# Packed attention and two MoE layers on one core: the first MoE's cosine argument carried in turns

## The chip, the cores and the metric

The kernel runs on one core of one Trainium2 chip. The metric is the device time of one execution in microseconds (us); the kernel before was run three times, with a median of 1744.01 us (1743.73 to 1751.22). The engines are named as the profile names them: PE is TensorE's matmul, PEld its weight load, DVE is VectorE, ACT is ScalarE, POOL is GpSimd, SP is SyncE.

## The reference

Eight batches of eight heads with 576 tokens go through an attention by way of 32 packs, and the 4608 tokens of 512 features that come out go through two MoE layers of 2048 inner features.

```python
def sm_attn(qq, kk, vv):                     # scale = 1/sqrt(64)
    s = scale * np.matmul(qq, kk.transpose(0, 1, 3, 2))
    s = s - np.max(s, axis=-1, keepdims=True)
    a = np.exp(s)
    return np.matmul(a / (np.sum(a, axis=-1, keepdims=True) + 1e-09), vv)

p_packed = sm_attn(p, k, v)
x = sm_attn(q, p_packed, p_packed)           # then tokens x (heads * 64)

h = x @ w_in                                 # first MoE
y = (h * np.cos(h)) @ w_out

h = y @ w2_in                                # second MoE
P = a[0] + a[1] * h + a[2] * h * h + a[3] * h * h * h
Q = 1.0 + np.abs(b[0]) * np.abs(h) + np.abs(b[1]) * h * h
out = (P / (Q + 1e-6)) @ w2_out
```

## The kernel before

Every float32 operand of a matmul is carried as two parts, hi and lo, and a product takes three matmuls (`PASSES`). The weights come as 64-bit words and are made into the two parts by `convert` (L74 to L93: Sign and Abs on ACT, four integer and float steps on DVE, two products on POOL, a copy on ACT).

The work falls into three stages. In the first, the packs attend to the tokens, and `wunit` (L279) multiplies the pooled packs with the first MoE's `w_in`, so that W' stands in for the second attention product and `w_in` together; W' leaves PSUM in `wev` (three of four pieces by ACT at L296, one by DVE at L294) and goes to HBM.

The second stage is the first MoE. Its 128 slots (8 batches, 2 halves of 288 tokens, 8 pairs of feature blocks) run in the loop of L609. A slot does 12 matmuls of 288 columns into h (`mm_h`, L530), the chain that makes g = h cos h out of them (`chain1`), and the 24 matmuls that add g to y (`mm_y`, L574) for the slot two back. h lies in two PSUM buffers (bufs=2), each of which comes free when the last reader of the chain, L561, is done. The chain is: L554 on ACT (u = h/(2 pi) + 0.25), L555 on DVE (u rounded by adding and taking away 1.5 * 2^23), L556 on DVE (r = h - 2 pi u), L560 on ACT (Sin of r + pi/2), L561 on DVE (g = h r). Then `finish_g` splits the g of the slot before into gh (L66, ACT) and gl (L67, DVE). Beside this the same engines do the second attention of the next batch (`attn2_steps`, whose splits run on POOL too), the splits of the next batch's W' (POOL), the conversion of the rest of `w_out` at the start, and from slot 16 on one conversion of the second MoE's weights every third slot (`conv_w2`).

The third stage is the second MoE (from L649), whose chain is another one.

The order on each engine is not written out by hand: the tile framework orders the instructions when it builds the program, from their dependencies, their place in the code and its own estimate of times, and each engine then runs its list in that order. Some instructions are held behind the latest matmul of `mm_h` (`hold`).

Of the kernel before, what the change touches and what calls it, by code (L numbers as in the profile page):

```python
# [12 lines left out]
AF = mybir.ActivationFunctionType  # L13
ALU = mybir.AluOpType
# [6 lines left out]
def pack_attention_moe_moe_kernel(  # L21
# [14 lines left out]
    nc = tc.nc  # L36
# [11 lines left out]
    scale = 1.0 / math.sqrt(D)  # L48
    RND = 1.5 * 2.0 ** 23
    INV2PI = 1.0 / (2.0 * math.pi)  # L50
    PASSES = ((0, 0), (0, 1), (1, 0))

    # Keeps an instruction behind the matmul `until` in the issue order.
    def hold(ins, until):
        if until is None:
            return
        tc.add_manual_dep(
            ins.ins,
            until.ins.name,
            mybir.DependencyInfo(mybir.DependencyClass.NoSync, mybir.DependencyReason.SCHED_ONLY),  # L60
            reason="issue order",
        )

    # A float32 operand is carried as two float32r parts, x = hi + lo (exact).
    def split(hi, lo, src, lo_eng, until=None):
        hold(nc.scalar.activation(out=hi, in_=src, func=AF.Copy), until)  # L66
        lo_eng.tensor_tensor(out=lo, in0=src, in1=hi.bitcast(F32), op=ALU.subtract)  # L67

    # The weights come as float64 words (viewed as integers).  The word's upper half gives sign,
    # exponent and 20 bits, its lower half the rest; together they give the two float32r parts.  # L70
    def words(w):
        return w.bitcast(U32).rearrange("p (n t) -> p n t", t=2)

# [32 lines left out]
    coef = const.tile([128, 8], F32, name="coef")  # L106
# [1 line left out]
    QC = 1.0 + 1e-6  # L108

    if True:  # L110
# [1 line left out]
        a_p = [ctx.enter_context(tc.tile_pool(name="a0", bufs=1))]  # L112
        RW = dict(reuse_waits="tile")
        wb_p = ctx.enter_context(tc.tile_pool(name="wb", bufs=1, side="right"))
# [27 lines left out]
        def load_kv(n):  # L142
# [10 lines left out]
            out=coef[:, 4:6], in0=par[:, 4:6], scalar1=-1.0, scalar2=None, op0=ALU.mult  # L153
        )
        nc.vector.tensor_tensor(out=coef[:, 4:6], in0=coef[:, 4:6], in1=par[:, 4:6], op=ALU.max)
        nc.vector.memset(coef[:, 6:7], 0.25)
        nc.vector.memset(coef[:, 7:8], math.pi / 2.0)
        nc.vector.memset(par[:, 6:7], QC)
        qb = par[:, 6:7]
# [119 lines left out]
        def wunit(P, hp, fq):  # L279
            ps = ps0.tile([128, 512], F32, tag="w", bufs=2, name="w")  # L280
            wl = wl_t[P]
            for i, (a, c) in enumerate(PASSES):
                nc.tensor.matmul(  # L283
                    out=ps,
                    lhsT=wl[a][:, hp].rearrange("p b m -> p (b m)"),
                    rhs=w1i_s[hp][c][:, 512 * fq:512 * fq + 512],
                    start=(i == 0),
                    stop=(i == 2),
                )
            if fq % 2 == 0:  # L290
                wev_t[P, hp] = wi_p.tile([128, 1024], F32, tag="wev", bufs=3, name="wev")
            o = wev_t[P, hp][:, 512 * (fq % 2):512 * (fq % 2) + 512]
            if fq % 4 == 3:
                nc.vector.tensor_copy(o, ps)  # L294
            else:
                nc.scalar.activation(out=o, in_=ps, func=AF.Copy)  # L296
            if fq % 2 == 1:
                t = wev_t.pop((P, hp))
                g, gg = divmod(hp, 2)
                for b2 in range(2):  # L300
                    nc.scalar.dma_start(
                        out=wd[2 * P + b2][g, 64 * gg:64 * gg + 64, 512 * (fq - 1):512 * (fq + 1)],
                        in_=t[64 * b2:64 * b2 + 64, :],
                    )

# [1 line left out]
        a_t = {}  # L307

        def attn2_steps(b, pool, psp, pst, psb, tg, now):
# [92 lines left out]
        for n in range(NG + 1):  # L402
            if n >= 3:
                next(at, 1)
            if n < NG:
                s1(n)
                if n + 2 < NG:
                    load_kv(n + 2)
            if n >= 1:
                pv(n - 1)  # L410
            for _ in range(2):
                if units:
                    wunit(*units.pop(0))
            if n + 1 < NG:
                prep(n + 1)
            if n < NG:
                et(n)
            for x in range(3 * n, 3 * n + 3):
                if 0 <= x < len(cv1):
                    conv_w1i(x)  # L420
            for _ in range(2):
                if units:
                    wunit(*units.pop(0))
            if n >= 1:
                ppt(n - 1)
                if n % (2 * G) == 0:
                    P = n // (2 * G) - 1
                    units += [(P, hp, fq) for hp in range(H // 2) for fq in range(4)]
# [7 lines left out]
            pass  # L436
        e0a.close()

# [1 line left out]
        e1k = ExitStack()  # L440
        wo_p = ctx.enter_context(tc.tile_pool(name="wq", bufs=1, **RW))
        w1o_s = {}
# [33 lines left out]
            nc.sync.dma_start(out=w2d[0][i], in_=hi.bitcast(F32))  # L476
            nc.sync.dma_start(out=w2d[1][i], in_=lo.bitcast(F32))

        # The second MoE's weights and tokens move in where the first one's leave.
        NB = NT // 512  # L480
        w2_s, x_t, pools = {}, {}, {}

# [57 lines left out]
        def finish_g(n):  # L540
            if n not in gl_t:
                return
            gt = gl_t.pop(n)
            gh = wk.tile([128, 2, HS], F32R, tag="gh", bufs=3, name="gh")
            gl = wk.tile([128, 2, HS], F32R, tag="gl", bufs=3, name="gl")
            split(gh, gl, gt, nc.vector)
            gs_t[n] = (gh, gl)

        def chain1(n):
            ph = h_t.pop(n)[:, :, 0:HS]  # L550
            u = wk.tile([128, 2, HS], F32, tag="u", bufs=2, name="u")
            r = wk.tile([128, 2, HS], F32, tag="r", bufs=2, name="r")
            gt = wk.tile([128, 2, HS], F32, tag="g", bufs=2, name="g")
            nc.scalar.activation(out=u, in_=ph, func=AF.Identity, scale=INV2PI, bias=coef[:, 6:7])  # L554
            nc.vector.tensor_scalar(out=u, in0=u, scalar1=RND, scalar2=RND, op0=ALU.add, op1=ALU.subtract)  # L555
            nc.vector.scalar_tensor_tensor(  # L556
                out=r, in0=u, scalar=-2.0 * math.pi, in1=ph, op0=ALU.mult, op1=ALU.add
            )
            finish_g(n - 1)
            nc.scalar.activation(out=r, in_=r, func=AF.Sin, bias=coef[:, 7:8])  # L560
            nc.vector.tensor_tensor(out=gt, in0=ph, in1=r, op=ALU.mult)  # L561
            gl_t[n] = gt

        def mm_y(n):
# [25 lines left out]
        for f in range(NFC):  # L590
            if f % 4 == 0:
                for _ in range(4):
                    wunit(*units.pop(0))
                load_wq(0, f // 4)
            conv_w1o(f)
            if f + 2 < NFC:
                load_w1o(f + 2)
            if f % 4 == 2:
                split_wq(0, f // 4, nc.gpsimd)
# [9 lines left out]
        for n, (b, hf, j) in enumerate(slots):  # L609
            s = hf * 8 + j  # L610
            mm_h(n)
            chain1(n)
            if n >= 2:
                mm_y(n - 2)
            i2, ph2 = divmod(n - 16, 3)
            if 0 <= i2 < 2 * NFC:
                if ph2 == 0:
                    load_w2(i2)
                elif ph2 == 2:
                    conv_w2(i2)  # L620
            if b + 1 < B:
                if s == 0:
                    at = attn2_steps(b + 1, at_p, psh, "h", 2, {"aT": ("qT", 1)}, lambda: last_h[0])
                if s % 2 == 1:
                    next(at, 1)
                if s == 15:
                    for _ in at:
                        pass
                for jj, (sl, ss) in enumerate(((2, 7), (10, 13), (12, 15), (14, 16))):
                    if s == sl:  # L630
                        load_wq(b + 1, jj)
                    if s == ss:
                        split_wq(b + 1, jj, nc.gpsimd, last_h[0])
            if b > 0 and s == 0:
                split_wq(b, 3, nc.gpsimd, last_h[0])
            move_in(n)
# [9 lines left out]
        for f in range(13, NFC):  # L646
            load_w2s(f, pools["b"])

# [1 line left out]
        slots2 = [(t, f) for t in range(NB) for f in range(NFC)]  # L650
        h2_t, g2_t, o_t = {}, {}, {}

# [127 lines left out]
```

## Time and profile before

| | |
|---|---|
| median of three runs | 1744.01 us |
| the profiled execution's own time (its span) | 1744.9 us |
| TensorE's mean granted clock | 0.973 of full speed |
| busy: PE, DVE, ACT, POOL | 93%, 82%, 67%, 20% of the span |
| first stage, first MoE, second MoE | about 0 to 205, 205 to 930, 930 to 1745 us |

A busy share is that of instructions in work; matmuls overlap, so that a stretch in which PE is busy throughout can still hold more or fewer matmuls. An instruction's busy time on DVE or POOL includes time in which it is started but held. "Idle before, releaser" is the time in which an engine stood still ahead of an instruction, and what ended it.

### The profile page before, as it was taken

The page shows a single profiled execution, that of the slowest core. Times are in us where ns is not written, and L with a number is a line of the kernel's source. Part 1 is how long each engine was busy: PE and PEld are TensorE (multiplying, and loading weights), DVE is VectorE, ACT ScalarE, POOL GpSimd, SP SyncE. Part 2 cuts the span into 40 slices and gives each one's busy share as a digit, 9 for nine tenths or more (in the row PEclk, how much of TensorE's full clock was granted, in tenths as well). Part 3 has the DMA queues.
Part 4 walks back from the last instruction along what each step waited for, and adds up shares of the span by engine and source line. Part 5 has one row for each costly group of instructions (what it writes and reads, how often), then busy time and mean ns, then how long its engine had stood idle before and what let it go on. Part 6 is the DMA issues. An engine that isn't in the chain of part 4 may idle for free.

```text
span 1744.9 us, 24418 instructions
## 1 busy us (share of the span) xinstructions
PE 1619.0 (93%) x8896; PEld 1419.4 (81%) x8896; DVE 1424.5 (82%) x2143; ACT 1175.8 (67%) x1917; POOL 355.0 (20%) x235
## 2 busy tenths in 40 slices
PE   5889578999899989899999999999999999999996
PEld 3668378989899989889898888888888888888884
DVE  6993598798889889988867888888888888888884
ACT  4554566666656566666547787878787878787874
POOL 4650553434334434343300000000000000000000
PEclk9989789999999999999999999999999999999998
DMA  9897822443434434433348020202020202020000
GB/s 291 249 258 234 271 88 83 135 134 113 141 120 134 135 122 136 140 129 107 130 161 304 1 72 1 72 1 73 1 73 1 73 0 72 2 72 1 31 19 25
DMA packets 99768, 183.52 MB, mean 105 GB/s; under 512 B 11584, under 2 KB 46400, under 8 KB 99648
## 3 DMA queue, kind: packets, MB, share of 16 engines
q1 hardware_dynamic: 92224, 163.09, 29.3%
q10 hardware_dynamic: 7424, 18.88, 3.5%
q8 instruction: 70, 1.15, 0.3%
q14 instruction: 50, 0.41, 0.1%
HBM read 117.97 MB, written 63.96 MB: 104 GB/s over the span
## 4 chain that ended last, share of the span: by engine, by line
PE 66%; DVE 20%; ACT 5%; issue 4%; DMA 3%; POOL 1%; SPq 0%; ACTq 0%; DVEq 0%
PE h L659 23%; PE o L718 23%; PE y L574 11%; PE h L530 6%; DVE gl L67 3%; DVE u L555 3%; DVE cvp L89 2%; DVE r L556 2%; DVE cvp L87 2%; DVE g L561 2%; DVE cvf L90 1%; DVE cvf L82 1%; DMA st<-in_moe_w_in_dram 1%; PE w L283 1%; PE s L209 1%
## 5 line engine op out<-in xcount | busy, mean ns | idle before, releaser
L574 PE MATMUL y<-gh,w1o 128*128 128x288 f32 x2048 | 431.8, 297 | 2.3 <-DVE yl L67 2.3
L659 PE MATMUL h<-x,w 128*128 128x512 f32 x1728 | 422.7, 393 | 0.0
L659 PEld LDWEIGHTS h<-x,w 128*128 128x128 f32 x1728 | 324.1, 188 | 74.2
L574 PEld LDWEIGHTS y<-gh,w1o 128*128 128x128 f32 x2048 | 338.1, 190 | 3.8 <-DVE yl L67 3.2
L718 PE MATMUL o<-w,g2h 128*128 128x512 f32 x1152 | 334.0, 394 | 1.3 <-ACT g2h L677 1.3
L574 PE MATMUL y<-gl,w1o 128*128 128x288 f32 x1024 | 298.7, 297 | 15.0 <-DVE gl L67 14.7
L530 PE MATMUL h<-ah,wq 128*128 128x288 f32 x1024 | 236.2, 307 | 46.0 <-DVE g L561 43.2
L718 PEld LDWEIGHTS o<-w,g2h 128*128 128x128 f32 x1152 | 216.0, 188 | 53.1 <-ACT g2h L677 2.1
L530 PEld LDWEIGHTS h<-ah,wq 128*128 128x128 f32 x1024 | 179.5, 197 | 51.0 <-issue 49.4
L574 PEld LDWEIGHTS y<-gl,w1o 128*128 128x128 f32 x1024 | 193.3, 189 | 18.9 <-DVE gl L67 18.9
L718 PE MATMUL o<-w,g2l 128*128 128x512 f32 x576 | 199.9, 393 | 0.0
L693 ACT ACTIVATE sq<-h 128x512 f32<-128x512 f32 x144 | 87.4, 607 | 155.7 <-PE h L659 155.6
L560 ACT ACTIVATE r<-r,coef 128x576 f32<-128x576 f32 x128 | 99.1, 775 | 103.1 <-DVE r L556 102.4
L695 DVE SCALAR_TENSOR_TENSOR ab<-sq,coef,ab 128x512 f32<-128x512 f32 x144 | 108.1, 751 | 67.8 <-ACT ab L694 67.5
L530 PE MATMUL h<-al,wq 128*128 128x288 f32 x512 | 156.1, 305 | 0.0
L67 DVE TENSOR_TENSOR gl<-g,gh 128x576 fp32r<-128x576 f32 x128 | 126.3, 989 | 18.0 <-ACT gh L66 16.3
L704 DVE SCALAR_TENSOR_TENSOR ab<-ab,y 128x512 f32<-128x512 f32 x144 | 99.5, 691 | 48.1 <-ACT y L701 47.5
L91 POOL TENSOR_TENSOR cvf<-cvf,cvs 128x512 f32<-128x512 f32 x64 | 88.2, 1377 | 217.7 <-DVE cvf L90 216.5
L554 ACT ACTIVATE u<-h,coef 128x576 f32<-128x576 f32 x128 | 93.8, 734 | 54.3 <-PE h L530 53.8
L718 PEld LDWEIGHTS o<-w,g2l 128*128 128x128 f32 x576 | 108.0, 188 | 25.6
L696 ACT ACTIVATE c<-h,coef 128x512 f32<-128x512 f32 x144 | 114.1, 792 | 9.8 <-DVE g2l L683 9.8
L561 DVE TENSOR_TENSOR g<-h,r 128x576 f32<-128x576 f32 x128 | 95.9, 750 | 30.1 <-ACT r L560 29.9
(97 smaller groups left out, 2775.6 us busy)
## 6 DMA issues: line engine op xcount, KB each, us to landing
x<-yd SPq DMA_DIRECT2D x36, 512.0 KB
w<-w2d SPq DMA_DIRECT2D x68, 256.0 KB
st<-in_moe_w_in_dram SPq DMA_DIRECT2D x32, 512.0 KB
wd<-wev ACTq DMA_DIRECT2D x64, 256.0 KB
st<-in_moe_w_out_dram SPq DMA_DIRECT2D x32, 512.0 KB
wq<-wd SPq DMA_DIRECT2D x32, 512.0 KB
kx<-in_k_dram SPq DMA_DIRECT2D x16, 576.0 KB
vx<-in_v_dram SPq DMA_DIRECT2D x48, 192.0 KB
```

The lines of the kernel that those rows point to most:

```text
L67: lo_eng.tensor_tensor(out=lo, in0=src, in1=hi.bitcast(F32), op=ALU.subtract)
L91: nc.gpsimd.tensor_tensor(out=ff, in0=ff, in1=sg, op=ALU.mult)
L530: last_h[0] = nc.tensor.matmul(out=ps[:, u, 0:HS], lhsT=wq[:, g, a, o:o + 128], rhs=a_t[b, g][c][:, hf * HS:hf * HS + HS], start=(i == 0), ...
L554: nc.scalar.activation(out=u, in_=ph, func=AF.Identity, scale=INV2PI, bias=coef[:, 6:7])
L560: nc.scalar.activation(out=r, in_=r, func=AF.Sin, bias=coef[:, 7:8])
L561: nc.vector.tensor_tensor(out=gt, in0=ph, in1=r, op=ALU.mult)
L574: nc.tensor.matmul(out=y_t[d][:, 0:HS], lhsT=w1o_s[f // 4][a][:, f % 4, 128 * d:128 * d + 128], rhs=gs[c][:, u], start=(f == 0 and i == 0) ...
L659: nc.tensor.matmul(out=ps, lhsT=w2_s[f][:, 0, a, 128 * kk:128 * kk + 128], rhs=x_t[t, c, kk], start=(i == 0), stop=(i == 3 * NKD - 1),)
L695: nc.vector.scalar_tensor_tensor(out=ab, in0=sq, scalar=coef[:, 5:6], in1=ab, op0=ALU.mult, op1=ALU.add)
L696: nc.scalar.activation(out=c1, in_=ph, func=AF.Identity, scale=coef[:, 3:4], bias=coef[:, 2:3])
L704: nc.vector.scalar_tensor_tensor(out=ab, in0=ab, scalar=QC, in1=y0, op0=ALU.add, op1=ALU.mult)
L718: nc.tensor.matmul(out=o_t[s], lhsT=g2_t[n][a][:, 128 * s:128 * s + 128], rhs=w2_s[f][:, 1, c], start=(f == 0 and i == 0), stop=(f == NFC ...
```

## The change

Three places are touched. In `wunit`, the copies that take W' out of PSUM scale it by 1/(2 pi): the ACT copy gets a scale, the DVE copy becomes a multiplication. All of h in the first MoE is then in turns. In `chain1`, L554 adds 1.5 * 2^23 to h on ACT (no scale, the constant comes from the column of `coef` that held 0.25), so that writing u as float32 rounds it to a whole number; L555 falls away; L556 becomes r = (u - 1.5 * 2^23) - h; a new ACT instruction makes |r|; Sin takes -2 pi |r| + pi/2, which is the cosine; and the last product becomes (2 pi h) * r, as a scalar-tensor-tensor instruction with the same two tensor inputs.

```diff
-        nc.vector.memset(coef[:, 6:7], 0.25)
+        nc.vector.memset(coef[:, 6:7], RND)
...
             if fq % 4 == 3:
-                nc.vector.tensor_copy(o, ps)
+                nc.vector.tensor_scalar(out=o, in0=ps, scalar1=INV2PI, scalar2=None, op0=ALU.mult)
             else:
-                nc.scalar.activation(out=o, in_=ps, func=AF.Copy)
+                nc.scalar.activation(out=o, in_=ps, func=AF.Copy, scale=INV2PI)
...
-            nc.scalar.activation(out=u, in_=ph, func=AF.Identity, scale=INV2PI, bias=coef[:, 6:7])
-            nc.vector.tensor_scalar(out=u, in0=u, scalar1=RND, scalar2=RND, op0=ALU.add, op1=ALU.subtract)
+            nc.scalar.activation(out=u, in_=ph, func=AF.Identity, bias=coef[:, 6:7])
             nc.vector.scalar_tensor_tensor(
-                out=r, in0=u, scalar=-2.0 * math.pi, in1=ph, op0=ALU.mult, op1=ALU.add
+                out=r, in0=u, scalar=RND, in1=ph, op0=ALU.subtract, op1=ALU.subtract
             )
             finish_g(n - 1)
-            nc.scalar.activation(out=r, in_=r, func=AF.Sin, bias=coef[:, 7:8])
-            nc.vector.tensor_tensor(out=gt, in0=ph, in1=r, op=ALU.mult)
+            nc.scalar.activation(out=r, in_=r, func=AF.Abs)
+            nc.scalar.activation(out=r, in_=r, func=AF.Sin, scale=-2.0 * math.pi, bias=coef[:, 7:8])
+            nc.vector.scalar_tensor_tensor(
+                out=gt, in0=ph, scalar=2.0 * math.pi, in1=r, op0=ALU.mult, op1=ALU.mult
+            )
             gl_t[n] = gt
```

## Rows read from the trace of the kernel before

**Rows 1.** The page: busy time by engine; granted clock in 40 slices (tenths).
```profile
PE 1619.0 (93%) x8896; PEld 1419.4 (81%) x8896; DVE 1424.5 (82%) x2143; ACT 1175.8 (67%) x1917; POOL 355.0 (20%) x235
...
PEclk9989789999999999999999999999999999999998
```

**Rows 2.** Stretches: length, busy (count) of PE, PEld, DVE, ACT, POOL; clock, DMA.
```profile
205.00:281.00 76.00, 51.40 (x338) 49.84 (x337) 70.42 (x90) 44.19 (x70) 42.06 (x28) 0.84 0.34 108
...
281.00:371.90 90.90, 89.85 (x672) 89.30 (x673) 74.19 (x117) 61.38 (x91) 28.18 (x16) 1.00 0.40 125
...
371.90:860.00 488.10, 450.49 (x3252) 442.27 (x3253) 435.35 (x598) 305.11 (x462) 196.12 (x113) 0.98 0.40 131
860.00:920.00 60.00, 60.00 (x455) 60.00 (x454) 35.95 (x56) 29.65 (x43) 0.00 (x0) 1.00 0.43 144
```

**Rows 3.** Waits from 205 to 945 us: total us, times, longest us.
```profile
ACT r L560 <- DVE r L556: 102.4, 77, 3.8
...
PE h L530 <- DVE g L561: 43.2, 17, 10.3
...
PE y L574 <- DVE gl L67: 14.7, 12, 4.6
```

**Rows 4.** DVE by line, 371.9 to 860 us: busy us, mean ns | idle before, releaser.
```profile
L67 DVE TENSOR_TENSOR gl<-g,gh 128x576 fp32r<-128x576 f32 x88 | 90.8, 1033 | 7.1 <-ACT gh L66 6.0
L556 DVE SCALAR_TENSOR_TENSOR r<-u,h 128x576 f32<-128x576 f32 x88 | 65.9, 749 | 5.7
L555 DVE TENSOR_SCALAR u<-u 128x576 f32<-128x576 f32 x88 | 65.6, 746 | 11.1 <-ACT u L554 11.1
L561 DVE TENSOR_TENSOR g<-h,r 128x576 f32<-128x576 f32 x87 | 65.2, 749 | 14.4 <-ACT r L560 14.2
```

**Rows 5.** Single lines, 250 to 880 us: duration ns minimum/median/maximum, first and last start.
```profile
L555 DVE TENSOR_SCALAR u<-u x113: 396/453/2660, 260.0 to 877.0; 128x576 f32<-128x576 f32 x113
...
L556 DVE SCALAR_TENSOR_TENSOR r<-u,h x113: 694/753/757, 265.1 to 877.5; 128x576 f32<-128x576 f32 x113
...
L67 DVE TENSOR_TENSOR gl<-g,gh x113: 689/752/2965, 253.1 to 875.9; 128x576 fp32r<-128x576 f32 x113
```

**Rows 6.** The line L555 alone, two stretches: length, DVE busy (count), clock, DMA.
```profile
205.00:281.00 76.00, 9.70 (x10) 0.84 0.34 108
...
371.90:860.00 488.10, 65.64 (x88) 0.98 0.40 131
```

**Rows 7.** ACT by line, 371.9 to 860 us.
```profile
L560 ACT ACTIVATE r<-r,coef 128x576 f32<-128x576 f32 x87 | 67.5, 775 | 76.3 <-DVE r L556 75.6
...
L66 ACT ACTIVATE gh<-g 128x576 fp32r<-128x576 f32 x88 | 59.7, 678 | 23.7 <-DVE g L561 23.2
...
L88 ACT ACTIVATE cvf<-cvf 128x512 f32<-128x512 f32 x28 | 17.6, 629 | 15.1 <-DVE cvp L87 15.0
...
L353 ACT ACT_TABLE_LOAD x5 | 6.4, 1283 | 0.1
L560 ACT ACT_TABLE_LOAD x5 | 6.4, 1283 | 0.1
```

**Rows 8.** Time order at one stop of PE: start us, us, instruction [idle before].
```profile
557.74 2.24 DVE L90 SCALAR_TENSOR_TENSOR cvf<-cvp,cvf 128x512 f32<-128x512 f32 x1
559.90 1.67 DVE L555 TENSOR_SCALAR u<-u 128x576 f32<-128x576 f32 x1
561.67 0.75 DVE L556 SCALAR_TENSOR_TENSOR r<-u,h 128x576 f32<-128x576 f32 x1
562.34 0.75 DVE L561 TENSOR_TENSOR g<-h,r 128x576 f32<-128x576 f32 x1
...
559.38 1.87 POOL L67 TENSOR_TENSOR al<-aT,ah 128x576 fp32r<-128x576 f32 x1
...
563.24 0.37 PE L530 MATMUL h<-ah,wq 128*128 128x288 f32 x1 [2.78 <-DVE g L561]
```

**Rows 9.** DVE's copy of W', whole run.
```profile
L294 DVE COPY wev<-w 128x512 f32<-128x512 f32 x16 | 11.0, 685 | 10.4 <-DMA wd<-wev 5.2 <-PE w L283 4.1 <-PE h L530 1.1
```

## The prediction

> **What bounds the kernel now.** I read the busy shares first: PE is at 93% and DVE at 82% of the span [rows 1], which says only that both matter. The stretches say where [rows 2]. From 860 to 920 us the first MoE runs with no attention and no weight conversion beside it: PE is busy throughout and starts 455 matmuls in 60 us, 131.9 ns each. That is the floor for this stage. By it the 3252 matmuls from 371.9 to 860 us need 428.9 us and take 488.1: 59.2 us are lost. From 205 to 281 us 338 matmuls need 44.6 us (a little more, since one or two are wider) and take 76: 31 us lost. From 281 to 371.9 us 672 need 88.6 and take 90.9: 2 us. The change touches the stage from 205 to 930 us, so some 93 us are the most that it can bring.
>
> The waits say who owes them [rows 3]: PE stops 17 times for DVE's g (L561, which frees the h buffer; 43.2 us) and 12 times for DVE's gl (14.7 us). The rest of the 93 is mostly clock: a mean granted clock of 0.98 over 488 us is 10 us, one of 0.84 over 76 us is 12 us, part of it while PE stood still anyhow [rows 2]. It falls to its lower level (1.2 of 2.4 GHz) behind such stops. DVE is busy 435.35 of 488.1 us there, 89%, and 93% in the first stretch; ACT is at 63% and 58%. So where PE loses time, DVE is what it waits for. The stretch between is the natural experiment: DVE at 82% and ACT at 68%, and PE loses almost nothing.
>
> **The change part by part.** Removed: L555, 128 times. Its median is 453 ns and its mean from 371.9 to 860 us 746, since some take up to 2660 [rows 4, 5]. The long ones lie beside a POOL instruction: one takes 1.67 us and ends 0.3 us after POOL's [rows 8]. gl does the same (752 to 2965), while L556, which reads h from PSUM, never takes over 757 [rows 5]. From 371.9 to 860 us the 88 L555 take 65.64 us [rows 6]: 88 x 0.453 = 39.9 of work and 25.8 of being held. The work goes for good. Of the hold a part only passes to the next such instruction (gl, or a conversion step); between none and all I take half, so DVE is relieved by 39.9 + 12.9 = 52.8 us and would have 382.5 left. From 205 to 281 us ten L555 take 9.70 us: 4.5 of work, 5.2 of hold; by halves 7.1.
>
> Added: the Abs on ACT, 128 times. Nearest in shape and kind is gh (128x576, no bias column): 678 ns; an existing Abs takes 629 ns for 512 elements [rows 7]; Sin with its bias column 775 is the upper bound. I take 678: 60 us in the 488, 87 us in all. ACT would go from 305 to 365 us there. The existing Abs run between Sins, and the tables are loaded five times each for L353 and L560, once per batch [rows 7]; 28 Abs cause no load, so the new ones cost none either.
>
> Exchanged at equal price: L556 keeps its form, two tensors of which one in PSUM. L561 becomes the form of L556 (both 749 ns [rows 4]). L554 loses a scale and keeps its bias column. DVE's 16 W' copies (685 ns [rows 9]) become scalar multiplications at the same shape out of PSUM; L556 at 749 for 576 elements bounds them to a few tens of ns, under 2 us in all. The 48 on ACT get an immediate scale: nothing, or at most the 97 ns that lie between Sin and gh [rows 7], 4.7 us, in a stretch where they wait for matmuls and DMAs. I take 0 for both. No DMA and no queue is moved. The memset costs the same.
>
> On the chain of one slot, with no queue ahead, L555's 0.46 us (and about 0.1 us to the next instruction [rows 8]) leave and Abs's 0.68 (and the same 0.1) come: h is freed some 0.2 us later. Where PE paces, two h buffers cover that: a slot has 36 matmuls, 36 x 131.9 ns = 4.75 us, and the chain's five instructions sum to 3.5 us with L554 taken like Sin [rows 4, 5, 7]. If that cover is gone it costs 0.2 us a slot. Where DVE paces, r starts in L555's place. At the stop shown, L90, L555 and L556 stand ahead of the g that PE waits for, so about 1.7 of its 2.78 us would go [rows 8].
>
> The sum. From 371.9 to 860 us: if DVE can only be filled to the 82% at which the middle stretch ran without loss, 382.5 us of work take 469 us, a gain of 19; if it stays as full as now (89%) they take 429, the floor, a gain of 59. ACT's 365 us would fill it to 80%, more than the 68% of that stretch, which is a reason not to take the upper end. I take a gain of 33, a little under the middle. From 205 to 281 us: 5, between 0 (the first slots wait behind weight conversion and a table load rather than L555) and 10. Middle stretch: 0 to 2, I take 0. Together 38 us. Against its own span that is 1744.9 - 38 = 1707; the median of the runs is 0.9 us below that span, so the forecast is 1706. What is late next is then gl, held beside POOL, and at some places ACT.
>
> **The rivals.** First, DVE is relieved fully and PE reaches its floor nearly everywhere: the upper bounds, 59 + 10 + 2 = 71 us, give 1673, so this case is 1660 to 1688. For it: all of PE's long waits name DVE. Against it: bursts of attention and conversion work stay.
>
> Second, nothing to be measured: the stops come from bursts in which DVE is held beside POOL, and not from the mean load. From 371.9 to 860 us POOL is busy 196 us [rows 2]. If all 25.8 us of hold pass to other instructions, and if in each burst L555's 453 ns are given back by Abs between r and g, the stops there stay as they are and only the 5 us of the first stretch come: 1739, or 1735 to 1753. For it: the conversion's L90, ahead of L555, took 2.24 us itself [rows 8]. Against it: L555 is itself among those held. (The Trainium skill, GPSIMD Engine Reference, "Key points", says that GpSimd shares its SBUF interfaces with VectorE, against instructions in a 2-port mode or with two SBUF inputs. The trace agrees, 757 against 2660 and 2965 ns [rows 5]; the page doesn't say whether the time held passes on, which is what this rival turns on.)
>
> Third, slower: ACT takes DVE's place. ACT runs its list in order and stands at its head for r for 102 us [rows 3]; busy 305 and idle 183 us make up its 488. With Abs it has 365 to do, so it becomes the pace once its idle time cannot shrink from 183 to 123 us, that is, when it still waits for r as long as now. gh and the next u stand behind Abs and Sin, and DVE's gl and PE behind these. The price: at each of the 29 stops [rows 3] another 0.68 us, 20 us, or 1764; this case runs from 1753 to 1775. Against it: r comes earlier by at least L555. (The Trainium skill, ScalarE: Activation LUTs, "Rules for kernel authors", says that simple elementwise work belongs on VectorE, not ScalarE. Row against row it is right about the instruction alone, 453 ns against 678; charged to all 128 slots that would be 29 us, 1773, this rival's end. It looks at the price of one instruction, not at which engine is full.)
>
> A rival that needs no price: that ScalarE's sum isn't rounded as meant. It would change values, not times.
>
> **How the numbers follow.** Forecast, 1688 to 1735 with 1706 as its centre: 0.55. To the floor, below 1688: 0.15. No change, within 1735 to 1753: 0.17. Slower, above 1753: 0.13. A measurement of this kernel can tell about 0.5% (9 us) from no change, so: faster 0.70, same 0.17, slower 0.13. The range is 1674 to 1755: it leaves out the lower half of the second of these cases and nearly all of the last, about 2 in 10. One thing widens every case: the framework orders the instructions anew, and another order moves single stops by 1 to 3 us either way.
>
> **What would show it.** Right: DVE's busy time in the stage falls by 60 to 90 us and ACT's rises by about 87; PE's waits for g and gl fall from 58 us to under 35; ACT's wait for r falls well below 102 us; the clock in the middle stretch rises towards 1.00; the stage ends 30 to 45 us earlier and the second MoE takes as long as now. gl's mean, 1033 ns, rises if the hold passes on. Wrong: PE's waits keep their sum while DVE's share drops (second rival), or PE waits for u or gh, or DVE for ACT's Sin much longer than 14 us [rows 4] (third). Abs with a table load of its own would break the price, and so would a new order that puts the weight conversion ahead of the chain.

## The result and the profile after

The changed kernel takes 1729.66 us (median; 1729.02 to 1730.22) against 1743.87: a ratio of 0.9909, with a 95% interval of 0.9888 to 0.9930. It is faster by 14 us, inside the range and on the side that was forecast, but the forecast was 38 us. The profiled execution's span went from 1744.9 to 1728.3 us, by 16.6.

The page after, to be read beside [rows 1]: 76 us of DVE's work are gone and 75 have come to ACT.

```profile
PE 1613.2 (93%) x8896; PEld 1414.8 (82%) x8896; DVE 1348.8 (78%) x2015; ACT 1250.9 (72%) x2045; POOL 354.8 (21%) x235
...
PEclk8889888999999999999999999999999999999998
```

To see where the 16.6 us lie, both traces are cut at the same work, not at the same time: at the first matmul of h of slot 0, of slot 24 and of slot 112. Between slots 24 and 112 all the loads that repeat are present: the next batch's attention and the conversion of the second MoE's weights. Each such stretch holds the same 3302 matmuls, which at 131.9 ns each need 435.5 us. Stretches of before (slots 0 to 24, 24 to 112), with the columns of [rows 2]:

```profile
205.20:349.78 144.58, 119.95 (x853) 118.34 (x852) 125.08 (x174) 90.60 (x137) 66.74 (x42) 0.92 0.36 115
349.78:845.60 495.82, 457.18 (x3302) 448.51 (x3301) 443.43 (x613) 311.64 (x470) 197.18 (x115) 0.98 0.41 132
```

The same stretches after:

```profile
205.44:353.72 148.28, 122.42 (x854) 120.68 (x852) 117.07 (x152) 104.69 (x162) 66.34 (x41) 0.90 0.35 112
353.72:828.86 475.14, 446.71 (x3302) 441.04 (x3301) 383.69 (x523) 359.81 (x555) 194.58 (x115) 0.99 0.42 134
```

Slots 24 to 112 became 20.7 us shorter, slots 0 to 24 became 3.7 us longer, and the rest is unchanged: h starts at 205.2 and 205.4 us, the last 16 slots take 85.7 and 86.0, and from the last y to the end it is 813.6 and 813.5 us. In the long stretch PE stands still for 28.4 us in place of 38.6 (length less busy time), which is half of the gain. The other half is shorter busy time, most of it clock: the same 3302 matmuls are busy for 446.7 us in place of 457.2, at a granted clock of 0.99 in place of 0.98. Two digits are coarse here: half of the time spent at the lower level (1.2 of 2.4 GHz) comes to 11.9 us before and 3.4 after, 8.5 of the 10.5 us.

The waits after, from 205 to 945 us, answer to [rows 3]:

```profile
DVE g L563 <- ACT r L562: 66.7, 66, 2.9
...
PE h L531 <- DVE g L563: 41.8, 18, 11.0
ACT r L561 <- DVE r L557: 35.7, 50, 2.7
...
PE y L578 <- DVE gl L67: 9.9, 6, 4.3
```

PE still waits 41.8 us for g (43.2 before), and 9.9 for gl (14.7 before). In slots 24 to 112 alone, its wait for g fell by 1.8 us (the table below) and that for gl by 4.9, as these lines of before and after show:

```profile
PE y L574 <- DVE gl L67: 10.1, 11, 1.7
...
PE y L578 <- DVE gl L67: 5.2, 4, 1.9
```

So the wait that the change was aimed at hardly moved. ACT waits for r 35.7 us in place of 102.4. In its place DVE now waits for ACT's Sin: 66.7 us, where it was 29.9.

DVE by line, slots 24 to 112 after, answers to [rows 4]; ACT by line in the same stretch, and the W' copy in the whole run, answer to [rows 7, 9]:

```profile
L67 DVE TENSOR_TENSOR gl<-g,gh 128x576 fp32r<-128x576 f32 x88 | 86.0, 977 | 10.5 <-ACT gh L66 9.7
L563 DVE SCALAR_TENSOR_TENSOR g<-h,r 128x576 f32<-128x576 f32 x88 | 66.1, 752 | 38.8 <-ACT r L562 38.1
L557 DVE SCALAR_TENSOR_TENSOR r<-u,h 128x576 f32<-128x576 f32 x88 | 65.7, 747 | 21.1 <-ACT u L556 21.0
...
L562 ACT ACTIVATE r<-r,coef 128x576 f32<-128x576 f32 x88 | 68.0, 772 | 1.1
...
L561 ACT ACTIVATE r<-r 128x576 f32<-128x576 f32 x87 | 59.2, 680 | 24.0 <-DVE r L557 24.0
...
L354 ACT ACT_TABLE_LOAD x6 | 7.7, 1283 | 0.1
L562 ACT ACT_TABLE_LOAD x6 | 7.7, 1283 | 0.1
...
L295 DVE TENSOR_SCALAR wev<-w 128x512 f32<-128x512 f32 x16 | 11.0, 685 | 10.6 <-PE w L283 7.2 <-DMA wd<-wev 3.4
```

Every price of a single instruction was right: Abs 680 ns (678 taken), g's new form 752, the scaled copies of W' 685 on DVE and 597 (median) on ACT as before, no table load for Abs (the two lines load 8 and 7 times in the whole run, before and after; [rows 7] has five of each because its stretch is shorter). What an instruction costs alone was not the error.

From the starts and ends of the instructions of each slot one can take the way from h to g apart. Means over slots 24 to 111, in us (the kernels of the lower lines come below):

| kernel | h done to u | u to r | r to Sin | Sin to g | h done to g done | slots over 7.8 | PE's wait for g |
|---|---|---|---|---|---|---|---|
| before | 0.73 | 2.33 | 0.32 | 0.67 | 7.06 | 34 | 22.9 |
| changed | 0.56 | 0.71 | 1.74 | 0.44 | 6.46 | 29 | 21.1 |
| neither L555 nor Abs | 0.91 | 1.04 | 0.34 | 0.60 | 5.79 | 10 | 8.7 |
| both L555 and Abs | 0.54 | 2.15 | 1.35 | 0.54 | 7.59 | 42 | 39.8 |
| changed, Abs twice | 0.75 | 0.56 | 3.16 | 0.28 | 7.74 | 42 | 48.2 |
| changed, conversion behind g | 0.67 | 0.88 | 1.56 | 0.33 | 6.43 | 14 | 8.6 |

("u to r" is from the end of the one to the start of the other, and so on; "slots over 7.8" counts those of the 88 slots in which g is done more than 7.8 us after h; PE's wait is the total in that stretch.) The change takes 1.62 us out between u and r, more than L555's 0.45 (0.75 on the mean, held time included), and puts 1.42 us in between r and Sin, more than Abs's 0.68. The last line shows that this mean is not all: with the same 6.4 us PE waits far less when the order differs. What counts is how many slots are late. With two buffers, a g has until the next h but one; between the two PE has some 60 matmuls, 7.9 us at 131.9 ns, and in the last 16 slots, where it hardly stops, 7.8 us pass (median). Where attention matmuls lie between it is more, so the count is a guide and not a price; but it goes with PE's wait where the mean does not. How Sin comes late can be seen at one stop of PE, in order of time, after:

```profile
469.60 0.68 ACT L561 ACTIVATE r<-r 128x576 f32<-128x576 f32 x1
471.83 0.64 ACT L88 ACTIVATE cvf<-cvf 128x512 f32<-128x512 f32 x1 [1.56 <-DVE cvp L87]
472.37 0.76 ACT L562 ACTIVATE r<-r,coef 128x576 f32<-128x576 f32 x1
...
469.17 2.63 DVE L87 TENSOR_SCALAR cvp<-cvf 128x512 uint32<-128x512 uint32 x1
471.83 1.80 DVE L89 TENSOR_TENSOR cvp<-st,cvp 128x512 f32<-128x512 uint32 x1
473.56 0.74 DVE L557 SCALAR_TENSOR_TENSOR r<-u,h 128x576 f32<-128x576 f32 x1
474.22 0.68 DVE L90 SCALAR_TENSOR_TENSOR cvf<-cvp,cvf 128x512 f32<-128x512 f32 x1
474.82 0.74 DVE L563 SCALAR_TENSOR_TENSOR g<-h,r 128x576 f32<-128x576 f32 x1
...
468.57 2.94 POOL L67 TENSOR_TENSOR wq<-wq 128x1024 fp32r<-128x1024 f32 x1 [4.27 <-ACT wq L66]
471.47 1.61 POOL L67 TENSOR_TENSOR al<-aT,ah 128x576 fp32r<-128x576 f32 x1
...
475.72 0.37 PE L531 MATMUL h<-ah,wq 128*128 128x288 f32 x1 [1.64 <-DVE g L563]
```

Abs ends at 470.28 us, and Sin could follow. The order that the framework made has a conversion step (L88) between the two, which waits for a DVE step that takes 2.63 us; Sin starts 2.1 us late. In 56 of the 128 slots Sin stands directly behind its Abs; in the others something stands between (in five of them only a table load).

But the late Sin is not what PE waits for at this stop. It is done at 473.13 us, while g starts at 474.82, and DVE does not stand still in between: in its list L87, L89, the next slot's r and L90 stand ahead of this g, the first two drawn out beside POOL's splits of W' and of the attention. What stands ahead of g on DVE makes this stop, so lateness on ACT and lateness on DVE have to be told apart by experiment.

### The profile page after: what moved, and what is told of

It is laid out like the page before. It is cut to its first block, busy times and chain, and to the rows that moved or that the text cites. A ratio compares the mean times of both kernels' runs of the same rounds, so it can differ in the third digit from the quotient of the medians.

```text
span 1728.3 us, 24216 instructions
## 1 busy us (share of the span) xinstructions
PE 1613.2 (93%) x8896; PEld 1414.8 (82%) x8896; DVE 1348.8 (78%) x2015; ACT 1250.9 (72%) x2045; POOL 354.8 (21%) x235
## 4 chain that ended last, share of the span: by engine, by line
PE 72%; DVE 13%; ACT 5%; issue 4%; DMA 4%; POOL 1%; SPq 0%; ACTq 0%; DVEq 0%; POOLq 0%
PE h L663 23%; PE o L722 23%; PE y L578 15%; PE h L531 8%; DVE cvp L89 2%; DVE cvp L87 2%; DVE gl L67 1%; DVE cvf L90 1%; DVE cvf L82 1%; DVE g L563 1%; PE s L193 1%; PE s L209 1%; DMA wd<-wev 1%; DVE r L557 1%; PE pv L249 1%
## 5 line engine op out<-in xcount | busy, mean ns | idle before, releaser
L531 PE MATMUL h<-ah,wq 128*128 128x288 f32 x1024 | 231.9, 302 | 43.0 <-DVE g L563 41.8
L531 PEld LDWEIGHTS h<-ah,wq 128*128 128x128 f32 x1024 | 175.6, 193 | 47.5 <-issue 47.0
L563 DVE SCALAR_TENSOR_TENSOR g<-h,r 128x576 f32<-128x576 f32 x128 | 96.1, 753 | 67.6 <-ACT r L562 66.7
L556 ACT ACTIVATE u<-h,coef 128x576 f32<-128x576 f32 x128 | 94.1, 736 | 65.6 <-PE h L531 65.2
L67 DVE TENSOR_TENSOR gl<-g,gh 128x576 fp32r<-128x576 f32 x128 | 120.8, 944 | 21.5 <-ACT gh L66 20.0
L557 DVE SCALAR_TENSOR_TENSOR r<-u,h 128x576 f32<-128x576 f32 x128 | 95.5, 747 | 36.9 <-ACT u L556 36.8
```

The source lines that it names most:

```text
L531: last_h[0] = nc.tensor.matmul(out=ps[:, u, 0:HS], lhsT=wq[:, g, a, o:o + 128], rhs=a_t[b, g][c][:, hf * HS:hf * HS + HS], start=(i == 0), ...
L556: nc.scalar.activation(out=u, in_=ph, func=AF.Identity, bias=coef[:, 6:7])
L557: nc.vector.scalar_tensor_tensor(out=r, in0=u, scalar=RND, in1=ph, op0=ALU.subtract, op1=ALU.subtract)
L563: nc.vector.scalar_tensor_tensor(out=gt, in0=ph, scalar=2.0 * math.pi, in1=r, op0=ALU.mult, op1=ALU.mult)
```

## The experiments

Two theories stood against each other. A: the gain was given back on ScalarE, by Abs and by what the order puts around it. B: the stops that are left come from conversion and attention steps ahead of g on VectorE, held beside GpSimd, whatever ScalarE does. Lengths are from the profiled executions, cut as above (slots 0 to 24, 24 to 112, and the stage from the first matmul of h to the end of the last of y; the expectations count to that matmul's start, 0.3 us less):

| kernel | median us | ratio to before (95%) | slots 0-24 | slots 24-112 | stage |
|---|---|---|---|---|---|
| before | 1743.87 | | 144.6 | 495.8 | 726.1 |
| changed | 1729.66 | 0.9909 (0.9888-0.9930) | 148.3 | 475.1 | 709.4 |
| e12 changed, again | 1733.37 | 0.9903 (0.9887-0.9920) | 148.0 | 475.4 | 709.4 |
| e1 neither | 1729.85 | 0.9876 (0.9844-0.9909) | 146.1 | 466.3 | 696.9 |
| e2 both | 1772.41 | 1.0108 (1.0054-1.0162) | 151.7 | 504.3 | 744.6 |
| e11 Abs twice | 1773.62 | 1.0138 (1.0118-1.0158) | 151.3 | 513.6 | 752.2 |
| e3 conversion behind g | 1720.12 | 0.9813 (0.9776-0.9850) | 147.4 | 461.0 | 694.4 |
| e7 before, conversion behind g | 1742.08 | 0.9961 (0.9946-0.9975) | 145.0 | 487.3 | 719.7 |
| e5 neither, conversion behind g | 1725.73 | 0.9866 (0.9844-0.9888) | 144.7 | 456.0 | 688.4 |
| e4 no GpSimd in that conversion | 1732.30 | 0.9887 (0.9853-0.9921) | 145.1 | 476.2 | 708.0 |
| e6 w_out converted in the slots | 1731.57 | 0.9901 (0.9876-0.9926) | 143.6 | 473.9 | 703.5 |
| e10 that, and both behind g | 1732.89 | 0.9904 (0.9886-0.9922) | 160.7 | 460.8 | 707.6 |
| e9 e3 and e6 together | 1715.89 | 0.9809 (0.9794-0.9824) | 144.4 | 461.2 | 691.6 |
| e8 e5 and e6 together | 1716.17 | 0.9806 (0.9790-0.9822) | 140.6 | 457.1 | 686.1 |

The stretches tell more than the totals, since the first stage, which ends before slot 0, took from 203 to 218 us in these executions. Its length differs for one and the same program: 205.4 us in the changed kernel's execution, 209.8 in its second one (e12).

**The changed kernel again.**

> The changed kernel once more, beside the others on one chip: 1729 to 1733 us, the stage 707 to 712 us, slots 24 to 112 in 473 to 477. It tells how far the stretches of one program repeat, and with that what differences between the kernels can carry.

```profile
209.81:357.81 148.00, 121.61 (x854) 119.87 (x852) 117.05 (x152) 104.58 (x162) 66.18 (x41) 0.91 0.34 112
357.81:833.20 475.39, 447.82 (x3303) 442.38 (x3301) 382.94 (x523) 359.25 (x555) 194.78 (x115) 0.99 0.41 134
```

Both stretches repeat within 0.3 us on another execution of this program; the median, 1733.37, lies just above what was expected. The long stretch also repeats between programs that are alike in it: 460.8 to 461.2 us in e3, e9 and e10, 475.1 and 473.9 in the changed kernel and e6, 456.0 and 457.1 in e5 and e8. Differences of a few us can be read from it, always with the order that the framework makes for each program. Slots 0 to 24 carry less: e4, whose edit touches only what runs there from slot 16 on, took 145.1 us against 148.3.

**Neither the rounding step nor Abs.**

```diff
-nc.vector.tensor_scalar(out=o, in0=ps, scalar1=INV2PI, scalar2=None, op0=ALU.mult)
+nc.vector.tensor_scalar(out=o, in0=ps, scalar1=INV2PI, scalar2=1.0 / 32.0, op0=ALU.mult, op1=ALU.add)
...
-nc.scalar.activation(out=r, in_=r, func=AF.Abs)
-nc.scalar.activation(out=r, in_=r, func=AF.Sin, scale=-2.0 * math.pi, bias=coef[:, 7:8])
+nc.scalar.activation(out=r, in_=r, func=AF.Sin, scale=-2.0 * math.pi)
...
-    out=gt, in0=ph, scalar=2.0 * math.pi, in1=r, op0=ALU.mult, op1=ALU.mult
+    out=gt, in0=ph, scalar=0.25, in1=r, op0=ALU.subtract, op1=ALU.mult
```

> The changed kernel without its Abs: W' gets 1/32 added to each element where it leaves PSUM, so that the eight heads' softmax rows, which each sum to one, add a quarter turn to h; Sin then takes -2 pi r of the shifted h directly, g is (h - 0.25) times it, and the 2 pi moves to where y is split. Neither the rounding step on VectorE nor Abs on ScalarE is left. Theory A (half of the gain was given back on ScalarE: Abs and what stands between it and Sin lie between r and g): another 15 to 30 us go, 1700 to 1715. Theory B (the stops that are left come from weight-conversion and attention steps that stand ahead of g in VectorE's order and are held beside GpSimd, whatever ScalarE does): 1724 to 1732, as with the change.

(Beside these lines, ACT's copies of W' get the same 1/32 as a bias, and the split of y takes the 2 pi.) The long stretch, and PE's wait for g in it:

```profile
364.23:830.54 466.31, 446.37 (x3302) 441.30 (x3301) 392.77 (x522) 303.21 (x468) 192.54 (x114) 0.99 0.42 137
...
PE h L531 <- DVE g L562: 8.7, 9, 2.0
```

In total nothing seems to come of it, as theory B says. But h starts at 218.2 us here: the first stage is 13 us longer, and that hides what the first MoE gains. In slots 24 to 112 Abs costs the changed kernel 475.1 - 466.3 = 8.8 us, less than the 15 to 30 that theory A expected. The longer first stage goes with the bias on the W' copies: the three kernels that have it (e1, e5, e8) show the three longest first stages, 214 to 218 us, against 203 to 212 in the other eleven, and e1's four runs agree (1728 to 1732 us), so it isn't one execution's. Why the bias makes it longer was not looked at.

**Both the rounding step and Abs.**

```diff
-nc.vector.memset(coef[:, 6:7], 0.25)
+nc.vector.memset(coef[:, 6:7], 0.0)
...
-nc.scalar.activation(out=r, in_=r, func=AF.Sin, bias=coef[:, 7:8])
+nc.scalar.activation(out=r, in_=r, func=AF.Abs)
+nc.scalar.activation(out=r, in_=r, func=AF.Sin, scale=-1.0, bias=coef[:, 7:8])
```

> The kernel before with Abs put in and its rounding step on VectorE kept (u rounded without the quarter, Abs of r, Sin of pi/2 - |r|): the addition alone. Theory A: ScalarE's extra 0.68 us a slot costs what it cost inside the change, 12 to 30 us, so 1756 to 1775. Theory B: ScalarE has room, 1740 to 1750.

```profile
363.89:868.23 504.34, 456.20 (x3302) 446.24 (x3301) 439.34 (x612) 366.16 (x558) 199.70 (x116) 0.98 0.40 130
...
PE h L530 <- DVE g L562: 39.8, 28, 4.0
```

Slower by 1.1%, as theory A expected. With e1 the square is full, and in slots 24 to 112 it adds up: taking L555 out is worth 495.8 - 466.3 = 29.5 us without Abs and 504.3 - 475.1 = 29.2 with it; putting Abs in costs 8.5 us beside L555 and 8.8 without it. In slots 0 to 24 it does not: there L555 is worth -1.5 us without Abs and 3.5 with it, and Abs costs 7.2 and 2.2.

**Abs twice.**

```diff
 nc.scalar.activation(out=r, in_=r, func=AF.Abs)
+nc.scalar.activation(out=r, in_=r, func=AF.Abs)
```

> The changed kernel with its Abs done twice over. In slots 24 to 112 Abs was worth 8.5 us on the kernel before and 8.8 on the changed one. If ScalarE's work between r and g has a price per us, a second Abs costs 8 to 12 us there again (483 to 487 us, 1740 in all). If the first one cost only by the order it happened to make, the second costs nothing or an amount of either sign: 470 to 478. If ScalarE becomes the pace with it (it would be at 95%), 20 us or more.

```profile
358.46:872.06 513.60, 461.52 (x3300) 452.81 (x3301) 384.73 (x523) 416.65 (x645) 192.45 (x113) 0.96 0.38 126
...
PE h L531 <- DVE g L564: 48.2, 18, 5.8
```

The first Abs cost 8.8 us, the second 38.5, with the same work of 0.68 us a slot. ACT isn't filled even so: it is busy for 416.65 of 513.6 us, 81%, and DVE for 75% (the 95% of the expectation doesn't follow either: 360 + 60 us in 475 are 88%). What grew is the way from r to Sin, from 1.74 to 3.16 us; h done to g done is 7.74 on the mean, just short of the 7.8 that the two h buffers cover, and longer than that in 42 of the 88 slots. PE also loses clock (0.96). So the 20 us or more that were expected came, but not for the reason given with them.

**The conversion behind g.** Only the order is touched: the last three DVE steps of a conversion wait in DVE's list until the g of the slot has been issued.

```diff
-nc.vector.tensor_scalar(out=pw, in0=f, scalar1=0x7F800000, scalar2=None, op0=ALU.bitwise_and)
+hold(nc.vector.tensor_scalar(out=pw, in0=f, scalar1=0x7F800000, scalar2=None, op0=ALU.bitwise_and), behind)
...
-nc.vector.scalar_tensor_tensor(
+last_g[0] = nc.vector.scalar_tensor_tensor(
     out=gt, in0=ph, scalar=2.0 * math.pi, in1=r, op0=ALU.mult, op1=ALU.mult
...
-convert(hi, lo, st_t.pop(("w2", i)), cv_p, 512, last_h[0])
+convert(hi, lo, st_t.pop(("w2", i)), cv_p, 512, last_h[0], last_g[0])
```

> The changed kernel with only the order touched: the last three VectorE steps of each conversion of the second MoE's weights are kept behind the g of the slot in which the conversion starts. Theory B: the stops of TensorE for g between 370 and 860 us (about 25 us of idle time, with the lower clock behind them some 35) mostly go, 1700 to 1715. Theory A: the order of the conversion matters little, 1724 to 1732.

```profile
350.80:811.82 461.02, 445.05 (x3302) 438.59 (x3301) 372.00 (x522) 362.01 (x557) 190.80 (x113) 1.00 0.42 140
...
PE h L531 <- DVE g L563: 8.6, 11, 1.7
```

The order alone is worth 14.1 us in this stretch. The median lies a little above the 1700 to 1715 of theory B; the mechanism is B's, for the stops that the change left: PE's wait for g fell from 21.1 to 8.6 us and the clock is at full speed. ACT's work is the same.

**The same order on the kernel before, and with neither.**

> The kernel before with the order alone touched: conversion of the second MoE's weights behind g, chain as it was. Slots 24 to 112 took 495.8 us before, 475.1 with the change, 461.0 with the change and this order. If stops come from the order whatever VectorE's load is, about 480 (as much as the 14 us there). If the load has to come down first, since VectorE is at 89% there, 490 to 500.

```profile
351.32:838.65 487.33, 447.75 (x3302) 438.86 (x3301) 437.27 (x610) 307.83 (x469) 198.39 (x114) 1.00 0.40 134
...
PE h L530 <- DVE g L561: 27.9, 21, 2.9
```

> The chain without rounding step and without Abs (the quarter turn in W') and, together with it, the conversion of the second MoE's weights behind g. So far the first MoE's stage (first matmul of h to last of y) took 725.9 us before, 709.2 with the change, 696.6 without Abs, 694.1 with the change and the conversion behind g. If the price of Abs and the order are two separate causes, both gains add: about 681 us. If they are one (Abs only hurts where a conversion step stands ahead of g), about 692.

```profile
359.81:815.82 456.01, 445.46 (x3303) 439.84 (x3301) 377.51 (x520) 303.16 (x467) 188.33 (x114) 1.00 0.42 139
```

The order is worth 8.5 us on the kernel before (487.3, between the 480 and the 490 that were to decide), 14.1 on the changed one and 10.3 without Abs. On the kernel before it does not take the stops away: PE stands still for 39.6 us in place of 38.6, and its wait for g grows from 22.9 to 27.9. All of the gain is busy time, 447.75 us in place of 457.2, at a granted clock of 1.00 in place of 0.98. On the changed kernel it is the other way round: PE stands still for 16.0 us in place of 28.4. So in these kernels the order removes stops only where DVE has less to do.

Abs costs 461.0 - 456.0 = 5.0 us once the order is mended, in place of 8.8. So order and Abs are in part two causes; some 4 us of Abs's price were the order's. The stage of e5 lies between the two values named for it.

**No GpSimd work in the conversion.**

```diff
-nc.gpsimd.tensor_tensor(out=ff, in0=ff, in1=sg, op=ALU.mult)
...
-nc.gpsimd.tensor_tensor(out=lo, in0=ff, in1=hi.bitcast(F32), op=ALU.subtract)
```

> The changed kernel with GpSimd's two steps left out of the conversion of the second MoE's weights (no sign, and the high part written in the low part's place, so the second MoE's values are others); VectorE's and ScalarE's steps stay. Theory B: 30 conversions hold VectorE no more beside 2.8 us of GpSimd work each, the held time of L87, L89 and gl falls from some 45 us to 25, and TensorE gets 10 to 20 us back: 1710 to 1720. Theory A: 1725 to 1732.

```profile
356.04:832.26 476.22, 449.85 (x3302) 444.17 (x3301) 371.52 (x522) 361.62 (x558) 113.57 (x55) 0.99 0.42 135
...
L90 DVE SCALAR_TENSOR_TENSOR cvf<-cvp,cvf 128x512 f32<-128x512 f32 x30 | 29.5, 982 | 0.6 <-ACT cvf L88 0.3
L89 DVE TENSOR_TENSOR cvp<-st,cvp 128x512 f32<-128x512 uint32 x30 | 26.8, 893 | 0.4
```

POOL's work fell from 194.6 to 113.6 us and DVE's from 383.7 to 371.5, but the stretch didn't get shorter (475.1, now 476.2). In the changed kernel L89 takes 1274 ns and L90 765 on the mean: L89's hold shrank, L90's grew. So 12 us less of busy time on DVE are worth nothing here, while another order of the same work is worth 14. That speaks against theory B's second half, that the hold beside GpSimd makes the stops, but doesn't settle it: POOL keeps the splits of W' and of the attention, the ones that draw out L87 and L89 at the stop shown above, and no run takes these away.

**The first slots: w_out's conversion.** e6 writes twelve of the sixteen conversions into the first six slots, e10 also holds them behind g.

```diff
 chain1(n)
+for f in (2 * n + 4, 2 * n + 5):
+    if f < NFC:
+        conv_w1o(f)
+        if f + 2 < NFC:
+            load_w1o(f + 2)
```

> The changed kernel with twelve of the sixteen conversions of w_out written into the first six slots of the first MoE instead of ahead of them. The first 24 slots took 144.6 us before and 148.3 with the change, though VectorE has 7 us less to do there. Theory C (their stops come from the order: conversion steps, written earlier, go ahead of the chain): 130 to 140 us for these slots. Theory D (the conversion itself is the pace of this stretch, as the first y needs all of it): 145 to 152.

```profile
210.82:354.42 143.60, 118.79 (x853) 116.83 (x852) 116.67 (x151) 104.60 (x162) 67.49 (x41) 0.93 0.34 112
```

> As the one above, and w_out's twelve conversions are kept behind g as well. Theory C (in the first 24 slots the order of conversion steps against g is what counts): 130 to 138 us for them, against 143.6 with the conversions merely written later. Theory D (the conversion itself is the pace there): 143 to 150.

```profile
208.19:368.88 160.69, 126.37 (x853) 123.84 (x852) 118.09 (x157) 106.28 (x164) 68.90 (x43) 0.89 0.32 105
...
PE y L580 <- ACT w1o L92: 11.6, 3, 6.6
```

Writing them later gives 4.7 us, between the two ranges; holding them behind g costs 12.4 against the changed kernel, beyond both ranges, and now PE waits for the converted weights themselves (11.6 us in three stops). That is nearer to theory D, in which the conversion is the pace of these slots: the order around it can give a few us, and putting it off costs more.

**Together.**

> The changed kernel with both orders: the conversion of the second MoE's weights behind g, and twelve of w_out's conversions in the first slots. Each alone shortened the first MoE's stage, from 709.2 us to 694.1 and to 703.2. If they touch different stretches they add: 688 us, some 1707 in all. If either only moved the stops elsewhere: 694 or more.

```profile
208.65:353.09 144.44, 119.68 (x854) 118.14 (x852) 118.29 (x152) 105.29 (x162) 68.30 (x42) 0.91 0.34 112
353.09:814.26 461.17, 445.19 (x3302) 438.66 (x3301) 372.09 (x522) 362.06 (x557) 190.65 (x113) 1.00 0.42 140
```

> All three together: no rounding step, no Abs, the conversion of the second MoE's weights behind g, and w_out's conversion in the slots. By theory C and with separate causes the stage takes some 665 to 672 us against 725.9 before, 1690 to 1700 in all; by theory D some 680, as without the last part.

```profile
214.08:354.66 140.58, 119.44 (x854) 118.73 (x852) 114.92 (x152) 88.01 (x138) 64.57 (x41) 0.92 0.35 117
354.66:811.80 457.14, 444.56 (x3303) 438.41 (x3302) 377.70 (x520) 303.08 (x467) 188.27 (x114) 1.00 0.42 139
```

e9 is the changed kernel with the two orders and takes 1715.89 us, 1.9% under the kernel before and 1.0% under the changed one measured beside it (1733.37). e8 goes without Abs, too, and has the shortest stage, 686.1 us; it ends at the same total, because its first stage is 5 us longer. Neither reached the values named for it: the stage is 691.6 us in e9 against 688, and 686.1 in e8 against 665 to 680. The two orders add only in part (in slots 0 to 24, e6's 4.7 us became 3.0 beside e3's order).

## Why the prediction was wrong, and where it was right

The reading of what bounds the kernel held: nearly all of the change lies in the first MoE, PE waits for DVE there, and of the 21.7 us that the long stretch before lost without standing still 11.9 are clock, which gave 8.5 of the 20.7 us gained. The prices held, as shown above.

**L555's worth: right.** The main term was 33 us from 371.9 to 860 us, between 19 and 59. By itself, without Abs, taking L555 out gives 29.5 us in slots 24 to 112. That it came so near to 33 is in part luck, since 33 was chosen between two bounds and not worked out. The relief of DVE was sized well: of the time held beside POOL, half had been assumed to pass on to others, 52.8 us in all; DVE's busy time fell by 59.7 us with the change (443.4 to 383.7) and by 50.7 in e1.

**Abs at no price: the step that failed.** The sum put 60 us of new work on ACT and charged it nothing, naming only a reason not to take the upper end; the 33 us were meant as the net gain. It costs 8.8 us there, measured from both sides of the square. The working had looked at ACT's share (63% going to 80%) and at the chain with no queue ahead (0.2 us, covered by two buffers, which it took for one slot's 4.75 us where they cover 7.8). But the chain was not 3.5 us long in this stretch: on the mean 7.06 us pass from h done to g done, because both engines serve others in between, and in 34 of 88 slots more than 7.8. A step that is moved to the other engine joins that engine's queue, and its real length is the wait that it brings: 1.42 us, not 0.68. The 2.33 us between u and r, of which L555 was 0.75, could be read from the trace before.

**The first stretch: wrong in sign.** Forecast 5 us of gain (and none from 281 us on), measured 3.7 of loss in slots 0 to 24. How it divides stays open: by way of e1 it is 1.5 for taking L555 out and 2.2 for Abs, by way of e2 a gain of 3.5 and a cost of 7.2, and another order alone moves these slots by some 3 us (e4). DVE was at 93% there, which I took for the pace. The prediction named the reason against it (the first slots wait behind weight conversion) as a lower bound of 0, and didn't follow it to a loss. The three stops of 10.3, 4.6 and 8.7 us are still there, at 11.0, 4.3 and 9.5; in the first and the third, conversion steps stand ahead of g on DVE, in the third attention steps as well. e10 shows that PE waits for the weights themselves once their conversion is put off.

So the sum that the runs give is 29.5 - 8.8 - 3.7 = 17 us, against 33 + 5 = 38: 21 us too much, of which 12.3 are in the long stretch (Abs 8.8, L555's worth 3.5) and 8.7 in the first one. The spans differ by 16.6.

**The signs.** DVE's fall came (76 us) and ACT's rise nearly so (75, not 87), ACT's wait for r fell as said, and the clock in the middle rose. PE's waits for g and gl fell only from 57.9 to 51.7 us, not under 35, and the stage ended 16.5 us earlier, not 30 to 45. Of the signs for the third rival one did appear: DVE's wait for Sin grew from 15 to 38 us in the long stretch. ACT's idle time there shrank to 475.1 - 359.8 = 115 us, past the 123 at which that rival had it stuck; e11, with ACT still only 81% busy, shows how little more it takes. This is also where the rule of the Trainium skill stands (ScalarE: Activation LUTs, "Rules for kernel authors": simple elementwise work to VectorE): beside a DVE that is busy for 89% it would have misled here, since the step taken off DVE was worth 29 us and the Abs put on ACT cost 9. The second Abs, which cost 38, takes nothing off DVE and doesn't test the rule.

**The second rival** put the stops down to bursts in which DVE is held. Half of it is right: what the change left are bursts, and e3 took 14 us of them away by order. That the hold makes them is not shown: e4 took 12 us off DVE for nothing, but the splits on POOL that also hold it stayed. Of the 25.5 us that e3 still lies above its 435.5 us of matmuls, 5 are Abs's; the rest wasn't taken apart.

## What to carry to other kernels

Where two engines hand one chain to and fro, price a step that moves by the time that passes at its place in the trace, queue and all, on the engine that it leaves and on the one that it joins; the instruction's own time is the smaller part on both. High busy shares on several engines say that there is a loss but not that unloading one gives it back: cut both traces at the same work, and look at which instruction stands ahead of the late one in its engine's list. If it isn't needed yet, its order may be worth nearly as much as the work that was taken out (14 and 21 us here).

## What the runs showed of the hardware

Three things had not been expected. Time held beside GpSimd doesn't simply pass to the next instruction, but it isn't simply gone either. With the change, L555's 66 us fell away, DVE's busy time fell by 59.7 us and gl's mean from 1026 to 977 ns, while L89's rose from 1101 to 1274. In e1, just as much without L555, DVE's busy time fell by 50.7 us, and gl took longer than before:

```profile
L67 DVE TENSOR_TENSOR gl<-g,gh 128x576 fp32r<-128x576 f32 x89 | 95.7, 1079 | 19.7 <-ACT gh L66 19.2
```

A second Abs of the same 678 ns cost more than four times the first (38.5 against 8.8 us in the stretch) with ACT at 81%. And a good part of what a kernel gains here is clock: the same 3302 matmuls were busy for 457.2, 446.7 and 445.05 us at granted clocks of 0.98, 0.99 and 1.00 (before, changed, e3), and e7 gained by this alone, 447.75 us at 1.00 with as much standing still as before.
